# TensorE's job work behind the transposes of its step instead of ahead of its scores, in a fused top-k attention and mixture-of-experts kernel

## The chip, the cores and the metric

One core of one Trainium2 chip. The metric is device time in microseconds (us) of one execution; lower is better. TensorE is PE in the rows (PEld its weight loads), VectorE DVE, ScalarE ACT, GpSimd POOL, SyncE SP.

## What is computed

The reference is attention over 8 batches of 8 heads, 576 rows of 64, that keeps only the 32 largest scores of each row, followed by a mixture of eight experts of which each token takes one. Cut to its core:

```
scores = scale * q @ k.T
kth    = the 32nd largest score of each row
attn   = softmax(where(scores >= kth, scores, -1e9))
x      = (attn @ v), heads side by side: 4608 tokens x 512
e      = argmax(x @ w_gate)            # one expert per token
out    = gate[e] * (relu(x @ w1[e]) @ w2[e])
```

## The kernel before, in words

**Two stages.** The attention comes first, the experts' products after it, all of one program. Between them a tail finishes the last attention steps and starts the first expert.

**The attention's steps.** The score rows are cut into tiles of 128 rows; two tiles make one step, and there are 144 steps, nine (NT) for each group of four heads, eighteen for a batch. The loop at L1014 writes step t's instructions out by hand, and each engine runs its own instructions in the order in which they are written. It works on different tiles at once, as a pipeline:

- TensorE, step t: the scores of tile pair t+3 (`scores`, L367), the products with v of pair t-5 (`av`, L477 and L492), the scores' last 64 columns (`scores_left`, L380 or L386), and the transposes of the masked scores of pair t-3 (`transp`, L461).
- ScalarE, step t: the exponentials of pair t-4 out of the transposes (`exps`, L467), the sign of score minus threshold for the two tiles of pair t-2 (`softmax`, L454), between these the copy of the new scores out of PSUM (L369), then the copy of their last columns (L388).
- GpSimd, step t: the threshold of pair t-1 (`nb`, L1017) and the masking additions of pair t-2 (L455, two per step).
- VectorE, step t: the 32 largest of pair t. 21 MAX8 over pieces of the scores (L1035), then rounds of MAX8 and MATCH_REPLACE8 over the candidates (L1043).
- SyncE stores the scores and loads q, k and v.

**The jobs.** Everything else of the attention is a job, a generator that `advance` (L902) moves on at the end of a step, in the order of due times, as far as estimated costs, free PSUM banks and limits allow. The jobs are: transposing the next q and k (`j_prep`), row sums and finished rows (`j_sums`, `j_rows`), and, once per batch, finding the one row that needs a second look, doing it again and storing it (`j_find`, `j_redo`, `j_patch`), and routing the batch's tokens (`j_route`). A job does not issue its compute instructions itself; it puts them into four lists: `pq` (TensorE), `aq` (ScalarE), `dq` (VectorE), `gq` (GpSimd). `flush` (L279) empties a list into the program. The job's DMAs go out where the job stands, except those that are in a list.

So what `advance` queues at the end of step t-1 is written out as follows: `gq` at once (L1069), `pq` at L1022 of step t, between the first and the second half of `softmax` and ahead of `scores`, `aq` at L1031 behind `transp`, and `dq` between the candidate rounds of step t (L1042 to L1046, from the third instruction on, or behind them). From step 144 on L1070 to L1074 advance the jobs and empty all four lists on the spot.

**Job work that matters here.** In `j_find` VectorE makes `r_key` (from GpSimd's counts `cnt`) and `r_ok`; TensorE multiplies `r_ok` (L640); ScalarE copies the product as `stat` (L642); and, in the same step as these two, VectorE reduces `mm` (L442) for the softmax's shift. In `j_route`, for one batch before the tail, TensorE sums `hist` (L868) and VectorE makes `skip` from it in the same step (L869). In `j_rows` VectorE reads TensorE's result one step after it was queued (`xm` and `lp`, L569 and L571), and the next TensorE piece goes into the bank that this read frees. `j_redo` has VectorE make `r_wk` (L719) out of two SBUF tensors. Scores go to one of seven buffers, three steps ahead of their use.

Of the kernel before, what the change touches and what calls it, by code (L numbers as in the profile page):

```python
# [48 lines left out]
def attention_moe(ctx, tc, q, k, v, w_gate, w1, w2, out):  # L49
# [211 lines left out]
    pq, aq, dq, gq = [], [], [], []  # L261
# [9 lines left out]
    def release(pt):  # L271
        free.append(pt)
# [6 lines left out]
    def flush(queue):  # L279
        while queue:  # L280
            queue.pop(0)()
# [15 lines left out]
    def bank():  # L297
        return free.pop(0)
# [43 lines left out]
    def grp(t):  # L342
        if t < 0 or t >= steps:
            return []
        n, s = divmod(t, NT)
        p = 2 * n
        if s < MAIN:
            return [p * NT + s, p * NT + MAIN + s]
        if s == MAIN:
            return [p * NT + 2 * MAIN, (p + 1) * NT + 2 * MAIN]  # L350
        s -= MAIN + 1
        return [(p + 1) * NT + s, (p + 1) * NT + MAIN + s]

    def scores(slot):

        if not slot:
            return
        EX.append(pair())
        for n, u in enumerate(slot):
            SB[u] = EX[-1][:, n]  # L360
            p, j = divmod(u, NT)
            assert p in READY
            h, i = divmod(j, MAIN)
            w = slice(2 * LEFT + i * 128, 2 * LEFT + (i + 1) * 128) if h < 2 else slice(0, 2 * LEFT)
            r = slice(h * D, (h + 1) * D) if h < 2 else slice(0, 128)
            qk = QK[p % 3][r]
            nc.tensor.matmul(MAINS[:, n], qk[:, 0, w], qk[:, 1, 2 * LEFT:], start=True, stop=True)  # L367

        nc.scalar.activation(bass.AP(EX[-1].tensor, EX[-1].offset, [list(EX[-1].ap[0]), [S + LEFT, 2], [1, M]]), MAINS,  # L369
                             AF.Copy)  # L370
# [66 lines left out]
    def spread(pt):  # L437
        pe(nc.tensor.matmul, pt[:, 0:128], top.to_broadcast([128, 128]), ident, start=True, stop=True)

    def settle(pt, ns, done):  # L440
        mm = jobs.tile([128, 1], F32, name="mm")
        vec(nc.vector.tensor_reduce, mm, pt[:, 0:128], axis=AX.X, op=OP.max)  # L442
        vec(done)
        for n in ns:
            vec(nc.vector.scalar_tensor_tensor, shift[:, n], slope, mm, level, op0=OP.mult, op1=OP.add)
# [3 lines left out]
    def softmax(t, us, i):  # L449
        b, lt = divmod(t, 2 * NT)  # L450
        if lt == 0 and i == 0:
            CNT[b] = jobs.tile([128, NLT], F32, name="cnt")
        nb, u = NB[t], us[i]
        nc.scalar.activation(upper(SG[i]), SB[u], AF.Sign, bias=nb[:, i, 1:2], accum_out=CNT[b][:, 2 * lt + i:2 * lt + i + 1])  # L454
        nc.gpsimd.tensor_tensor(SB[u], SB[u], SG[i], op=OP.add)  # L455

    def transp(t):
        x = EX[t].rearrange("p a s -> p (a s)")
        tt = three.rearrange("p (c q) -> p c q", c=NB9)
        for c in range(NB9):  # L460
            nc.tensor.matmul(tt[:, c], x[:, c * 128:(c + 1) * 128], ident, start=True, stop=True,  # L461
                             is_transpose=True)

    def exps(t):
        ET[t] = work.tile([128, NB9, 128], F32, name="et")
        assert t // NT in SHIFTED
        nc.scalar.activation(ET[t], three.rearrange("p (c q) -> p c q", c=NB9), AF.Exp, bias=shift[:, t // NT, 0:1],  # L467
                             scale=0.125)

    def av(t, us):  # L470
        et = ET[t]

        def one(px, p, h, n, q, kbs):
            rv = VV[p // 2]
            for kb in range(kbs):
                blk = MAIN if kb == MAIN else n * (MAIN + 1) + kb
                yield lambda kb=kb, blk=blk: nc.tensor.matmul(  # L477
                    px[h * 64:(h + 1) * 64], block(rv, p % 2, kb if kb < MAIN else MAIN + n, h), et[:, blk, q],
                    start=(kb == 0), stop=(kb == KB - 1))

        def both(a, b):
            for x, y in zip(a, b):
                x()
                y()

        p, j = divmod(us[0], NT)
        if j < 2 * MAIN:
            px = PX[:, (j % 2) * 128:(j % 2 + 1) * 128]
            both(*(one(px, p, h, h, slice(0, 128), MAIN) for h in range(2)))

            o = (MAIN + 1) * D
            nc.tensor.matmul(px, VV[p // 2][:, p % 2, o:o + 2 * D], et[:, MAIN, :], start=False, stop=True)  # L492
            if p not in XT:
                XT[p] = jobs.tile([128, S], F32, name="xt", bufs=4)
            if j % 2:
                act(nc.scalar.activation, XT[p][:, (j - 1) * 128:(j + 1) * 128], PX, AF.Copy)
        else:
            XT[p + 1] = jobs.tile([128, S], F32, name="xt", bufs=4)
            for n in range(2):
                px = PX[:, n * LEFT:(n + 1) * LEFT]  # L500
                both(*(one(px, p + n, h, n, slice(h * LEFT, (h + 1) * LEFT), KB) for h in range(2)))
                act(nc.scalar.activation, XT[p + n][:, 512:S], px, AF.Copy)
# [394 lines left out]
    def start(lane, job, due=0):  # L897
        lanes[lane].append((due, job))
        if len(lanes[lane]) == 1:
            wants[lane] = next(job)  # L900
# [36 lines left out]
    def prep(p):  # L937
        if p < P:
            start(f"prep{p % 2}", j_prep(p))
# [74 lines left out]
    for t in range(steps + LAG + TD + 4):  # L1014
        n, s = divmod(t, NT)
        if delayed:
            delayed[0](*delayed[1])  # L1017
        if grp(t - LAG - TD - 1):
            exps(t - LAG - TD - 1)
        if grp(t - LAG):  # L1020
            softmax(t - LAG, grp(t - LAG), 0)
        flush(pq)  # L1022
        scores(grp(t + LA))
        if grp(t - LAG):
            softmax(t - LAG, grp(t - LAG), 1)
        if grp(t - LAG - TD - 2):
            av(t - LAG - TD - 2, grp(t - LAG - TD - 2))
        scores_left(grp(t + LA))
        if grp(t - LAG - TD):
            transp(t - LAG - TD)  # L1030
        flush(aq)  # L1031
        one, two, last = topk(t, grp(t)) if grp(t) else ([], [], None)
        for m in range(max(len(one), 1)):
            if m < len(one):
                one[m][0](*one[m][1])  # L1035
        delayed = last
        if t == 1:
            settle(first_pt, [0, 1, 2, 3], lambda: release(first_pt))
            mine_, dq[:] = dq[:], []
            flush(mine_)  # L1040
        mine, dq[:] = dq[:], []
        for m, (f, a) in enumerate(two):  # L1042
            f(*a)  # L1043
            if mine and m >= 2:
                mine.pop(0)()
        flush(mine)  # L1046
        if t == 0:
            nc.vector.tensor_reduce(top, VQ[0][:, 0:2, 0], axis=AX.X, op=OP.max)
            first_pt = bank()
            spread(first_pt)  # L1050
            pq.pop()()
        if s == NT - 1 and n in MX:
            pool(nc.gpsimd.tensor_scalar, top, MX.pop(n), top, None, op0=OP.max)
        m = t - LAG + 1
        if m > 0 and m % (2 * NT) == 0:
            start("find", j_find(m // (2 * NT) - 1), t + DUE['find'])
            start("redo", j_redo(m // (2 * NT) - 1), t + DUE['redo'])
        m = t - LAG
        if 0 <= m < steps and m % NT == NT - 1:
            start("sums", j_sums(m // NT), t + DUE['sums'])  # L1060
            if m == steps - 1 and len(lanes["sums"]) == 1:

                for _ in range(2):
                    wants["sums"] = next(lanes["sums"][0][1])
                flush(gq)
                flush(aq)
        if t < steps:
            advance(s=s)
            flush(gq)  # L1069
        else:  # L1070
            for _ in range(TAIL if t < steps + TADV else 0):
                advance(None)
                for queue in (gq, pq, aq, dq):
                    flush(queue)  # L1074
        for at, job, a in AHEAD if first else ():
            if t - steps == at:
                job(*a)
        m = t - LAG - TD - 3
        if m >= 0 and m % NT == NT - 1:
            start("rows", j_rows(m // NT), t + DUE['rows'])  # L1080
        if s == PA:
            prep(2 * n + 4)
        if s == PB:
            prep(2 * n + 3)
        if s == LQ and n + 2 < NQ:
            load_qk(n + 2)
        if s == LV and 0 < n < NQ:
            load_v(n)
# [418 lines left out]
```

## Time and profile before

| | |
|---|---|
| median of 3 runs | 1328.07 us (1327.75 to 1328.79) |
| the profiled execution | 1328.21 us, of which the profile's span is 1326.4 us |
| TensorE, VectorE busy in the span | 92%, 78% |
| GpSimd, ScalarE busy in the span | 65%, 63% |
| TensorE's mean granted clock | 0.972 of full speed |

How to read it: the span is what the profiler saw of the program; 1.8 us of the execution lie outside. Busy shares are means over the two stages, so a stage is read from its own stretch. A row of a timeline says start, length, engine, source line, operation and tiles (written <- read), how many instructions are merged, and, in brackets, how long the engine stood idle before and who released it.

### The profile page before, as it was taken

Reading aid. Unit: us, or ns where it says so; the run is one execution under the profiler, and the core shown is the slowest. Engines: PE = TensorE matmul, PEld = TensorE weight load, DVE = VectorE, ACT = ScalarE, POOL = GpSimd, SP = SyncE. Lnnn points to the kernel's source line nnn. Section 1 sums busy time; section 2 is a strip of 40 time slices with the busy share of each in tenths; the row PEclk is TensorE's granted clock in tenths of the full one; section 3 lists DMA queues with packets and bytes.
Section 4 is the critical chain, followed back from the end, with each engine's and each line's share of the span. In section 5 each row is a group of like instructions: output and inputs, shape, how many; then the busy total and the mean of one; then the engine's idle time right before and its main releaser. Section 6 shows DMA issues by size and latency. Waiting matters only on the chain.

```text
span 1326.4 us, 31779 instructions
## 1 busy us (share of the span) xinstructions
PE 1220.1 (92%) x9126; PEld 975.1 (74%) x9126; DVE 1028.7 (78%) x6889; ACT 833.8 (63%) x1691; POOL 866.6 (65%) x1317
## 2 busy tenths in 40 slices
PE   5898989989899999989988859998899999999997
PEld 2576767767667667666666657887799899988996
DVE  7998999999999999999999965644673333345665
ACT  3998888988888798888887843432233323233442
POOL 3677766877877777877877966764654334255654
PEclk8999999999999899999999978998999999999999
DMA  6655554655555556556553524635564333256774
GB/s 173 207 176 182 173 182 149 185 163 165 177 158 167 159 172 176 167 159 173 180 164 123 177 62 134 207 93 160 151 183 151 112 104 120 82 154 187 219 216 124
DMA packets 271240, 211.19 MB, mean 159 GB/s; under 512 B 136215, under 2 KB 214215, under 8 KB 271056
## 3 DMA queue, kind: packets, MB, share of 16 engines
q1 hardware_dynamic: 260320, 185.92, 47.7%
q0 software_dynamic: 9504, 22.86, 5.4%
q8 instruction: 74, 1.21, 0.4%
q14 instruction: 110, 0.90, 0.2%
q10 hardware_dynamic: 1232, 0.30, 0.1%
HBM read 102.49 MB, written 107.90 MB: 159 GB/s over the span
## 4 chain that ended last, share of the span: by engine, by line
PE 42%; DVE 33%; ACT 9%; POOL 6%; issue 5%; DMA 3%; SPq 1%; another core or an unknown queue 0%; POOLq 0%; ACTq 0%; DVEq 0%
DVE cand L1035 16%; PE ph L1169 15%; PE y L1184 14%; DVE cand L1043 6%; DVE vq L1043 5%; PE ps L367 3%; PE pt L265 3%; ACT sg L454 3%; ACT sb L369 2%; PE px L477 2%; ACT et L467 2%; POOL sb L455 2%; PE tt L461 1%; PE mt L1149 1%; POOL wl L967 1%
## 5 line engine op out<-in xcount | busy, mean ns | idle before, releaser
L455 POOL TENSOR_TENSOR sb<-sb,sg 128x576 f32<-128x576 f32 x288 | 365.5, 1282 | 87.7 <-ACT sg L454 71.8
L1035 DVE MAX8 cand<-sb 128x8 f32<-128x52 f32 (+2 forms) x3024 | 368.4, 207 | 0.9 <-ACT sb L369 0.5
L967 POOL TENSOR_TENSOR wl<-r,wh 128x512 fp32r<-128x512 f32 x110 | 142.3, 1295 | 226.1 <-DVE wh L966 221.8
L454 ACT ACTIVATE sg<-sb,nb 128x576 int8<-128x576 f32 x288 | 225.6, 783 | 5.8 <-POOL sb L455 5.2
L477 PEld LDWEIGHTS px<-et,rv 128*64 128x64 f32 x2688 | 136.7, 145 | 122.3 <-issue 59.5
L1170 ACT ACTIVATE hh<-ph 128x320 fp32r<-128x320 f32 (+3 forms) x136 | 58.3, 429 | 241.7 <-PE ph L1169 226.8
L369 ACT ACTIVATE sb<-ps 128x1024 f32<-128x1024 f32 x144 | 148.1, 1028 | 76.7 <-PE ps L367 75.7
L1043 DVE MAX8 vq<-cand 128x8 f32<-128x22 f32 (+7 forms) x1152 | 193.6, 198 | 0.3 <-DVE vq L1043 0.3
L367 PE MATMUL ps<-qk 64*128 64x512 f32 (+1 forms) x576 | 188.3, 662 | 3.0 <-ACT sb L369 2.6
L467 ACT ACTIVATE et<-tt,shift 128x1152 f32<-128x1152 f32 x144 | 177.0, 1229 | 13.9 <-PE tt L461 13.8
L1171 DVE SCALAR_TENSOR_TENSOR hl<-ph,hh 128x320 fp32r<-128x320 f32 (+3 forms) x136 | 65.1, 478 | 151.2 <-ACT hh L1170 133.3
L477 PE MATMUL px<-et,rv 128*64 128x128 f32 (+1 forms) x2688 | 170.4, 275 | 11.8 <-ACT r_et L265 7.0
L461 PE MATMUL tt<-turner,sb 128*128 128x128 f32 x1296 | 168.4, 275 | 4.3 <-POOL sb L455 3.2
L1169 PE MATMUL ph<-xh,wh 128*128 128x320 f32 (+3 forms) x536 | 168.9, 315 | 0.0
L1169 PE MATMUL ph<-xh,wl 128*128 128x320 f32 (+3 forms) x536 | 165.3, 308 | 0.0
L1169 PE MATMUL ph<-xl,wh 128*128 128x320 f32 (+3 forms) x536 | 165.3, 308 | 0.0
L461 PEld LDWEIGHTS tt<-turner,sb 128*128 128x128 f32 x1296 | 147.6, 143 | 7.1 <-POOL sb L455 4.6
L1043 DVE MATCH_REPLACE8 cand<-vq,cand 128x22 f32<-128x22 f32 (+2 forms) x864 | 148.9, 178 | 0.0
L1184 PE MATMUL y<-wh,hl 128*128 128x512 f32 x324 | 128.4, 396 | 0.0
L1184 PE MATMUL y<-wh,hh 128*128 128x512 f32 x324 | 127.7, 394 | 0.6 <-ACT yo L1188 0.6
L1184 PE MATMUL y<-wl,hh 128*128 128x512 f32 x324 | 127.9, 395 | 0.0
L1169 PEld LDWEIGHTS ph<-xh,wh 128*128 128x128 f32 x536 | 101.6, 189 | 3.8 <-issue 0.9
(266 smaller groups left out, 2235.7 us busy)
## 6 DMA issues: line engine op xcount, KB each, us to landing
r<-in_moe_w_dram SPq DMA_DIRECT2D x220, 256.0 KB
sc<-sb SPq DMA_DIRECT2D x128, 288.0 KB
sc<-sb SPq DMA_DIRECT2D x128, 256.0 KB
rv<-in_v_dram SPq DMA_DIRECT2D x32, 256.0 KB
xs<-xm SPq DMA_DIRECT2D x16, 512.0 KB
rq<-in_q_dram SPq DMA_DIRECT2D x60, 128.0 KB
rk<-in_k_dram SPq DMA_DIRECT2D x60, 128.0 KB
sc<-sb SPq DMA_DIRECT2D x32, 144.0 KB
```

Source lines behind the costliest of these rows:

```text
L367: nc.tensor.matmul(MAINS[:, n], qk[:, 0, w], qk[:, 1, 2 * LEFT:], start=True, stop=True)
L369: nc.scalar.activation(bass.AP(EX[-1].tensor, EX[-1].offset, [list(EX[-1].ap[0]), [S + LEFT, 2], [1, M]]), MAINS, AF.Copy)
L454: nc.scalar.activation(upper(SG[i]), SB[u], AF.Sign, bias=nb[:, i, 1:2], accum_out=CNT[b][:, 2 * lt + i:2 * lt + i + 1])
L455: nc.gpsimd.tensor_tensor(SB[u], SB[u], SG[i], op=OP.add)
L461: nc.tensor.matmul(tt[:, c], x[:, c * 128:(c + 1) * 128], ident, start=True, stop=True, is_transpose=True)
L467: nc.scalar.activation(ET[t], three.rearrange("p (c q) -> p c q", c=NB9), AF.Exp, bias=shift[:, t // NT, 0:1], scale=0.125)
L477: yield lambda kb=kb, blk=blk: nc.tensor.matmul(px[h * 64:(h + 1) * 64], block(rv, p % 2, kb if kb < MAIN else MAIN + n, h), et[:, blk, q] ...
L967: (nc.gpsimd if i else nc.vector).tensor_tensor(lo, r, hi, op=OP.subtract)
L1035: one[m][0](*one[m][1])
L1043: f(*a)
L1169: nc.tensor.matmul(ph, a[:, c, :], x[:, c, s], start=(m == 0), stop=(m == len(seq) - 1))
L1184: nc.tensor.matmul(PY[u, t], a[:, s], x, start=(f == 0 and m == 0), stop=(f == FC - 1 and m == 2))
```

## The change

The line that empties TensorE's list moves, within the same step, from ahead of `scores` to behind `transp`, in front of the line that empties ScalarE's. No other line changes.

```
--- before.py
+++ after.py
@@ -1019,7 +1019,6 @@
             exps(t - LAG - TD - 1)
         if grp(t - LAG):
             softmax(t - LAG, grp(t - LAG), 0)
-        flush(pq)
         scores(grp(t + LA))
         if grp(t - LAG):
             softmax(t - LAG, grp(t - LAG), 1)
@@ -1028,6 +1027,7 @@
         scores_left(grp(t + LA))
         if grp(t - LAG - TD):
             transp(t - LAG - TD)
+        flush(pq)
         flush(aq)
         one, two, last = topk(t, grp(t)) if grp(t) else ([], [], None)
         for m in range(max(len(one), 1)):
```

## Rows read from the trace of the kernel before

**Rows 1.** Busy time by stretch: us, then PE, PEld, DVE, ACT, POOL, granted clock, DMA.
```profile
450.00:500.00 50.00, 46.49 (x422) 34.68 (x420) 50.00 (x405) 45.91 (x97) 40.10 (x68) 0.97 0.59 177
...
1000.00:1326.00 326.00, 317.85 (x1875) 286.25 (x1873) 147.69 (x257) 107.48 (x217) 148.84 (x152) 0.99 0.50 147
```

**Rows 2.** Waits of VectorE, 30 to 785 us: total us, times, longest.
```profile
DVE r_key L265 <- POOL cnt L265: 6.3, 2, 5.2
DVE mm L265 <- ACT stat L265: 6.2, 6, 1.6
DVE skip L265 <- PE pt L265: 2.7, 1, 2.7
DVE cand L1035 <- ACT sb L369: 0.5, 1, 0.5
```

**Rows 3.** Timeline of the first steps, TensorE, ScalarE and VectorE.
```profile
25.26 1.07 PE L265 MATMUL pt<-turner,rq 128*128 128x128 f32 x2 [7.20 <-DMA rq<-in_q_dram]
27.30 3.62 PE L367 MATMUL ps<-qk 128*128 128x512 f32 x4
30.95 1.02 ACT L369 ACTIVATE sb<-ps 128x1024 f32<-128x1024 f32 x1 [12.30 <-PE ps L367]
33.17 0.78 ACT L454 ACTIVATE sg<-sb,nb 128x576 int8<-128x576 f32 x1
```

**Rows 4.** Timeline around the two waits of r_key.
```profile
108.83 1.28 POOL L455 TENSOR_TENSOR sb<-sb,sg 128x576 f32<-128x576 f32 x1 [0.68 <-ACT sg L454]
113.86 0.20 DVE L265 SCALAR_TENSOR_TENSOR r_key<-cnt,idx 128x36 f32<-128x36 f32 x1 [5.18 <-POOL cnt L265]
...
199.62 1.28 POOL L455 TENSOR_TENSOR sb<-sb,sg 128x576 f32<-128x576 f32 x1 [1.95 <-ACT sg L454]
206.62 0.20 DVE L265 SCALAR_TENSOR_TENSOR r_key<-cnt,idx 128x36 f32<-128x36 f32 x1 [1.11 <-POOL cnt L265]
```

**Rows 5.** Waits of ScalarE, 32 to 109 us and then 109 to 781 us.
```profile
ACT sb L369 <- PE ps L367: 1.4, 2, 1.2
...
ACT sb L369 <- PE ps L367: 58.0, 40, 4.0
```

**Rows 6.** Timeline of one job step in which TensorE waits for VectorE.
```profile
382.89 1.18 PE L265 MATMUL pt<-turner,xt 128*128 128x144 f32 x8 [2.45 <-DVE lp L265]
386.45 1.02 ACT L369 ACTIVATE sb<-ps 128x1024 f32<-128x1024 f32 x1 [3.02 <-PE ps L367]
```

**Rows 7.** Timeline, one of the six mm chains: product, stat, mm.
```profile
400.56 0.18 PE L265 MATMUL pt<-r_ok,before 128*128 128x1 bf16 x1 [0.72 <-DVE r_ok L265]
405.25 0.17 ACT L265 ACTIVATE stat<-pt 128x3 f32<-128x3 f32 x1
405.45 0.29 DVE L265 TENSOR_REDUCE mm<-pt 128x1 f32<-128x128 f32 x1 [0.81 <-ACT stat L265]
```

**Rows 8.** Timeline of TensorE, scores of two steps with no job between.
```profile
115.03 1.13 PE L367 MATMUL ps<-qk 64*128 64x512 f32 x4
118.73 1.13 PE L367 MATMUL ps<-qk 64*128 64x512 f32 x4
```

**Rows 9.** Timeline around the wait of skip.
```profile
721.11 0.18 PE L265 MATMUL pt<-hist,ones 128*128 128x8 bf16 x1
721.35 0.16 DVE L265 TENSOR_SCALAR skip<-pt 128x1 f32<-128x1 f32 x1 [2.74 <-PE pt L265]
```

**Rows 10.** Instructions on tile r_wk: ns min/median/max; then the longest, in the timeline.
```profile
L265 DVE TENSOR_TENSOR r_wk<-sg,r_sb x8: 748/1022/5418, 182.4 to 836.6; 128x576 f32<-128x576 bf16 x8
...
763.22 2.52 POOL L455 TENSOR_TENSOR sb<-sb,sg 128x576 f32<-128x576 f32 x2
763.56 5.42 DVE L265 TENSOR_TENSOR r_wk<-sg,r_sb 128x576 f32<-128x576 bf16 x1
765.84 2.52 POOL L455 TENSOR_TENSOR sb<-sb,sg 128x576 f32<-128x576 f32 x2
```

**Rows 11.** Timeline of TensorE, the first instructions of the experts' stage.
```profile
806.63 0.63 PE L1149 MATMUL mt<-turner,kt 128*128 128x128 f32 x4
```

More of the change, by code (lines that the diff above doesn't have):

```diff
@@ L1021, in attention_moe @@
             softmax(t - LAG, grp(t - LAG), 0)
-        flush(pq)
         scores(grp(t + LA))
@@ L1030, in attention_moe @@
             transp(t - LAG - TD)
+        flush(pq)
         flush(aq)
```

## The prediction

> **What bounds the kernel now.** I read the busy time by stretch first. In the attention VectorE is busy 50.00 of 50 us, TensorE 46.5, ScalarE 45.9, GpSimd 40.1; in the experts' stage TensorE is, with 318 of 326 us [rows 1]. So the attention's length is VectorE's work and VectorE's waits, whatever TensorE gains by itself. The change touches TensorE's list alone, and that list is used this way only in the attention; the experts' stage, which begins at 806.6 us [rows 11], can only be shifted. Next I read VectorE's own waits. Between 30 and 785 us they are 6.3 us in two waits for GpSimd's counts, 6.2 us in six waits of `mm`, 2.7 us in one wait of `skip`, and 0.5 us, once, for scores [rows 2]. These 15.7 us are what a better order can win on VectorE directly. That scores were late only once also tells that bringing scores earlier, which is what the change does in each step, is worth nothing by that way: they stand ready in their buffers. Last I read what sets each of these waits, in the timelines.
>
> **The change part by part.** Nothing is added or removed: the same TensorE instructions, the same on every other engine, no DMA moved. TensorE has, in turn, a step's own work S and job work P, before and after. What shifts is which P stands between two S: it is now one S later. A step without jobs lasts 118.73 - 115.03 = 3.7 us [rows 8], so each P comes some 3.7 us later beside its S, and each S earlier by the P and the waits that stood ahead of it. What P waits for (VectorE's and ScalarE's job work of the step before) gets 3.7 us of slack; what waits for P in its own step loses 3.7.
>
> 1. The start, 0.5 us won. In step 1 the job's transposes wait 7.2 us for a load, and the scores stand behind them: they start at 27.30, ScalarE stands 12.3 us for them, and its first sign, at 33.17, comes only behind that [rows 3]. Now the scores go ahead of the wait. The transposes still end at 27.3, ScalarE's job copy of them follows (half as wide as the 1.02 us copy in these rows, so some 0.6 us), and the first sign starts near 28, some 5.2 us earlier. VectorE's 0.5 us wait for scores [rows 2] falls here and goes. Bounds: 0 and 0.5.
>
> 2. The waits of `r_key`, 5.5 us won. The first is 5.18 us at 113.86 and ends when GpSimd has made the counts; GpSimd's addition ahead of them, at 108.83, waited for ScalarE's sign [rows 4]. Between 32 and 109 us ScalarE waits only 1.4 us for scores [rows 5]: it is full and never makes up for its late start. So its 5.2 us of step 1 arrive whole, and nearly all of the 5.18 goes. The second, 1.11 us, hangs on an addition that waited 1.95 us for ScalarE [rows 4], and ScalarE waits 58 us for scores in the rest of the attention [rows 5]. I take 0.4 of it. Bounds: 0 (GpSimd late on its own account) and 6.3.
>
> 3. TensorE's waits in P, nothing won by themselves. In the job step shown TensorE waits 2.45 us for VectorE's reading of the bank, and ScalarE 3.02 us for the scores behind it [rows 6]. This goes; what hides it is VectorE, which is full. It matters through items 2 and 4 alone: ScalarE and GpSimd come earlier. Next late, in ScalarE's steps, are then its own copies of P, which now wait for P. The exponentials behind them must wait for the transposes ahead of P anyway, so the copies cost P and themselves on ScalarE; VectorE's lead in scores [rows 2] covers that. If the cover were gone, it would be up to the 3.0 us that ScalarE loses in [rows 6], in each such step.
>
> 4. `mm`, 3 us won. The product of `r_ok` stands in P, `stat` in ScalarE's list, `mm` behind it, all in one step. Here 4.7 us lie between the product and `stat` (405.25 - 400.56, the shortest of the six) [rows 7], because ScalarE's turn comes late, so 3.7 us more for P are covered with 1.0 to spare: no loss. How much earlier ScalarE's turn comes the trace does not show. Bounds: all 6.2 us won, or 3 us lost, if TensorE's step ends half a microsecond behind ScalarE's turn at each of the six. I take half the 6.2, since the lead of item 3 is as large as the single waits but is not had at each of the six.
>
> 5. `skip`, 1 us lost. Here nothing covers: TensorE's product is at 721.11, `skip` at 721.35, after 2.74 us of waiting [rows 9]. P one S later would make it 3.7 us longer; as TensorE has lost its waits by then, up to the whole 2.74 could go instead. I take 1 us of loss, nearer to the uncovered end. Behind the waiting instruction stand the rest of VectorE's selection and all its later steps, so it counts in full.
>
> 6. VectorE's stretched instructions, 1 us won. `r_wk` takes 748 ns at best, 1022 at the median and 5418 once, at 763.56, where GpSimd's four additions run without a gap from 763.22 to 768.36 [rows 10]. GpSimd comes earlier, so the same block should lie partly ahead of `r_wk`. Bounds for this one: 4.7 us won, nothing. The other stretched ones get a new phase each, of either sign; I take zero.
>
> The sum: -0.5 - 5.5 - 3 + 1 - 1 = -9.0 us on VectorE. The tail hangs on VectorE's end and the experts on the tail, so it goes through. Against the profiled execution of 1328.2 us (span 1326.4 and 1.8 outside), which is 0.1 above the median, this gives **1319.2 us**.
>
> **The rivals.** *A, nothing to measure, about 1327.6.* GpSimd's late counts come from its own work, `mm` from ScalarE's turn, and the gains stay on engines that do not bound: only the 0.5 us of item 1 is left. For it: VectorE is full [rows 1], TensorE is not. Against it: the late start of ScalarE [rows 3] is as large as the first wait of `r_key` [rows 4], and ScalarE has no gap in which the lag could come from elsewhere [rows 5].
>
> *B, slower, about 1337.* When ScalarE no longer waits between its two signs, GpSimd's two additions of a step follow each other without a gap, 2.5 us instead of twice 1.25 [rows 10], and VectorE's job instructions on two SBUF tensors stand still for the whole of it, as `r_wk` did for 5.42 us. The place is the redo, find and route work of VectorE, some four such instructions in each of seven batches. If half of them are stopped for one more addition of 1.25 us, that is 7 x 2 x 1.25 = 17.5 us, less the 9.0 above: +8.5. It comes out as slower from (9.0 + 2.7) / 7 = 1.7 us per batch. Against it: with GpSimd nearer to VectorE's pace its additions fall on the MAX8 of the next step, where the trace shows no stretch. The Trainium skill (SBUF — State Buffer, "SBUF: two separate sides") says that VectorE and GpSimd share one pair of SBUF ports under an exclusive lock, held for a whole instruction, so that the loser blocks fully. The trace agrees in the 5.42 us; by that rule B's 17.5 us come or stay away with the alignment of the two engines.
>
> *C, larger, about 1310.* All of the 15.7 us of waits but the 2.7 of `skip`, and the 4.7 of `r_wk`, go: 13.0 + 4.7 = 17.7. It needs ScalarE ahead at all six `mm`.
>
> **How the numbers follow.** A measurement of this kernel tells about 0.2%, 2.7 us, from no change: faster is below 1325.4, slower above 1330.7. My forecast with C has 0.68 (C 0.10 of it), A 0.18, B 0.14. The range goes from C, 1309, to 1331: A lies in it, and of B the part in which the stalls just outweigh the gain; what is left out is most of B and the gains beyond C.
>
> **What would show it.** Step 1: scores near 18 and the first sign near 28 us. `r_key` without its 5.18 us; waits of VectorE for GpSimd under 1 us. The waits of TensorE for `lp` gone, and ScalarE's 58 us for scores down to a fraction. `mm` at or below 0.8 us each, `skip` near 3.7. `r_wk` at 763 (now some 8 us earlier) below 5 us. The experts' stage begins near 798 and lasts as long as before. I am wrong if `r_key` still waits with the first sign at 28 (then GpSimd bounds it), if `mm` waits for TensorE rather than for ScalarE, if VectorE's job instructions get longer in sum by more than 9 us (B), or if the tail between VectorE's last selection and the experts grows by what the attention won.

## The result and the profile after

The changed kernel takes 1312.16 us (median of 4 runs, 1308.99 to 1314.04) against 1328.43 (4 runs, 1327.75 to 1330.23) beside it: a ratio of 0.9873, interval 0.985 to 0.9897, or 16.3 us. The prediction was 1319.2, 9.0 us less than before. The profiled execution of the changed kernel took 1314.04 us with a span of 1312.2, that is 14.2 less than the span before.

The attention is where it went. VectorE's last selection starts, with its 21 MAX8 over the scores (L1035), at 771.79 us before (first line) and at 756.39 after (second line), 15.4 us earlier:
```profile
771.79 2.56 DVE L1035 MAX8 cand<-sb 128x8 f32<-128x52 f32 x21
756.39 2.56 DVE L1035 MAX8 cand<-sb 128x8 f32<-128x52 f32 x21
```
The tail and the experts only follow: TensorE's first instruction of the experts' stage comes 15.9 us earlier [rows 11], and the time between those two points is nearly the same in both (34.8 us and 34.3). The experts' stage itself lasts 521.5 us, 1.7 more than before, so that 14.2 of the 15.9 us are left in the span.

The start, TensorE and ScalarE, in the timeline of the changed kernel:
```profile
18.45 1.98 PE L367 MATMUL ps<-qk 128*128 128x512 f32 x4 [0.48 <-ACT sb L369]
25.14 0.96 PE L265 MATMUL pt<-turner,rq 128*128 128x128 f32 x2 [3.87 <-DMA rq<-in_q_dram]
28.15 0.77 ACT L454 ACTIVATE sg<-sb,nb 128x576 int8<-128x576 f32 x1
...
790.70 1.09 PE L1149 MATMUL mt<-turner,kt 128*128 128x128 f32 x4
```
The scores now go ahead of the wait for `rq`, and the first sign stands at 28.15 instead of 33.17 [rows 3]. They also take 1.98 us instead of 3.62: before, they came behind TensorE's wait of 7.2 us, and the granted clock was 0.5 there, that is 1.2 GHz instead of 2.4.

VectorE's waits, 30 to 785 us, and the row of the longest one (columns as in [rows 2]):
```profile
DVE r_key L265 <- POOL cnt L265: 8.6, 2, 7.2
DVE skip L265 <- PE pt L265: 5.3, 1, 5.3
...
DVE mm L265 <- ACT stat L265: 2.2, 1, 2.2
...
773.49 0.20 DVE L265 SCALAR_TENSOR_TENSOR r_key<-cnt,idx 128x36 f32<-128x36 f32 x1 [7.21 <-POOL cnt L265]
```
The 7.21 us lie at 773, behind the last selection: that is the tail, which the earlier end only drew into the window. In the attention itself 1.36 (`r_key`) + 5.34 (`skip`) + 2.15 (`mm`) = 8.9 us of waiting are left of 15.7 [rows 2].

What the other two engines wait for, from the waits of ScalarE (109 to 770 us) and of TensorE (30 to 770 us):
```profile
ACT sg L454 <- POOL sb L455: 53.2, 42, 5.0
...
PE tt L461 <- POOL sb L455: 24.0, 36, 4.3
```
The waits have mostly changed their name. ScalarE's 58 us for scores [rows 5] have become 53 us for GpSimd's additions, and TensorE's 24 us for `lp` (one of these waits in [rows 6]) have become 24 us for the same additions. The two engines are little less idle than before: from 30 us to VectorE's last selection ScalarE stands 92 us instead of 102, TensorE 53 instead of 62. They are *earlier* against VectorE, and now stand in front of GpSimd.

TensorE's waits had a second price, its clock. Between the start and VectorE's last selection the granted clock of the kernel before falls to 0.5 (1.2 GHz) eight times; seven of these times begin within 2 us behind a wait of TensorE of 2.2 to 2.7 us, five of the waits being for `lp` (four more such waits were followed by no fall). In the changed kernel it falls once. No run separates the clock's share in the gain; a high clock alone is not enough for it: the run with a longer TensorE (below) has a mean granted clock of 0.984, above the 0.981 of the changed kernel, and is 13 us slower than that.

Out of one batch's chain from `r_key` to `mm`, in the timeline of the changed kernel:
```profile
294.23 2.53 POOL L455 TENSOR_TENSOR sb<-sb,sg 128x576 f32<-128x576 f32 x2
295.67 1.13 DVE L265 SCALAR_TENSOR_TENSOR r_key<-cnt,idx 128x36 f32<-128x36 f32 x1
298.81 0.17 ACT L265 ACTIVATE stat<-pt 128x3 f32<-128x3 f32 x1
301.32 0.28 DVE L265 TENSOR_REDUCE mm<-pt 128x1 f32<-128x128 f32 x1
301.77 0.36 DVE L265 SCALAR_TENSOR_TENSOR shift<-slope,mm,level 128x3 f32<-128x3 f32 x1
```
`stat` is 2.5 us ahead of `mm`, where before `mm` stood waiting for it [rows 7]. But `r_key`, which needs 0.20 us [rows 4], takes 1.13 here. It ends at 296.80; GpSimd's two additions, which follow each other without a gap, end at 296.76. Before, the same thing happened to other instructions, as in the timeline of the kernel before behind the `mm` of [rows 7]:
```profile
405.84 0.80 POOL L265 TENSOR_TENSOR vq<-vq 128x288 f32<-128x288 f32 x1
...
405.91 0.75 DVE L265 SCALAR_TENSOR_TENSOR shift<-slope,mm,level 128x3 f32<-128x3 f32 x1
```
`shift` ends at 406.66, the GpSimd operation at 406.64. So there are two accounts on VectorE, waits and lengthened instructions. I added up the 389 job instructions of VectorE (L265) between 30 us and its last selection in each timeline: 136.5 us before, 129.1 after. Those that are more than 0.08 us longer than the shortest of their kind, 42 before and 37 after, all end at one short distance behind the end of a GpSimd operation: 0.06 us or less, `hist` 0.2, `r_wk` 0.6.

| VectorE, us (negative is a gain) | forecast | measured |
|---|---|---|
| start (wait for scores) | -0.5 | -0.5 |
| waits of `r_key` | -5.5 | -4.9 (5.18 to 1.36, 1.11 to none) |
| waits of `mm` | -3 | -4.0 (6.2 to 2.2) |
| wait of `skip` | +1 | +2.6 (2.74 to 5.34) |
| length of the job instructions | -1 | -7.4 |
| the rest of the 15.4 | | -1.2 |

The measured figures are of one execution of each kernel. The first wait of `r_key`, 1.36 us here, is 2.53 us in the run with `skip` covered (below), whose program is the same up to there.

The last measured line but one is made of +4.9 for `r_key` (six batches at 1.1 us), -3.2 for `r_wk`, -3.2 for `pos`, -2.0 for `r_v`'s first, -1.9 for `shift`, -1.0 for `r_fl`, -0.9 for `sh`, and smaller ones.

`skip` and the `r_wk` of the last batch, in the timeline of the changed kernel:
```profile
700.96 2.57 PE L461 MATMUL tt<-turner,sb 128*128 128x128 f32 x9 [4.28 <-POOL sb L455]
704.72 2.08 PE L367 MATMUL ps<-qk 64*128 64x512 f32 x4
710.02 0.18 PE L265 MATMUL pt<-hist,ones 128*128 128x8 bf16 x1
710.30 0.16 DVE L265 TENSOR_SCALAR skip<-pt 128x1 f32<-128x1 f32 x1 [5.34 <-PE pt L265]
...
750.44 2.52 POOL L455 TENSOR_TENSOR sb<-sb,sg 128x576 f32<-128x576 f32 x2
752.34 1.23 DVE L265 TENSOR_TENSOR r_wk<-sg,r_sb 128x576 f32<-128x576 bf16 x1
```
The product for `skip` stands behind a whole step of TensorE's own work, 5.3 us from 704.72 to 710.02, and VectorE waits for all of it. About 1 us of this step is the clock: behind TensorE's wait of 4.28 us for GpSimd's additions the granted clock is 0.5 from 700 to 706 us, and the scores take 2.08 us where they take 1.13 at 2.4 GHz [rows 8]. `r_wk` now comes 0.6 us before the end of GpSimd's additions instead of at their beginning [rows 10], so it loses 0.5 us where it lost 4.7.

### The profile page after: what moved, and what is told of

It reads as the page before. It is cut to its first block, busy times and chain, and to the rows that moved or that the text cites. A ratio compares the mean times of both kernels' runs of the same rounds, so it can differ in the third digit from the quotient of the medians.

```text
span 1312.2 us, 31782 instructions
## 1 busy us (share of the span) xinstructions
PE 1218.0 (93%) x9126; PEld 969.5 (74%) x9126; DVE 1021.8 (78%) x6889; ACT 831.2 (63%) x1691; POOL 865.1 (66%) x1317
## 4 chain that ended last, share of the span: by engine, by line
DVE 40%; PE 37%; POOL 7%; issue 6%; ACT 6%; DMA 2%; SPq 1%; POOLq 0%; ACTq 0%; DVEq 0%
DVE cand L1035 19%; PE ph L1169 15%; PE y L1184 15%; DVE cand L1043 8%; DVE vq L1043 7%; POOL sb L455 2%; ACT sg L454 2%; PE pt L265 2%; PE mt L1149 1%; PE ps L367 1%; POOL wl L967 1%; ACT sb L369 1%; POOL table L857 1%; PE tt L461 1%; PE px L477 1%
## 5 line engine op out<-in xcount | busy, mean ns | idle before, releaser
L1035 DVE MAX8 cand<-sb 128x8 f32<-128x52 f32 (+2 forms) x3024 | 368.6, 208 | 0.3 <-issue 0.2
L477 PEld LDWEIGHTS px<-et,rv 128*64 128x64 f32 x2688 | 130.6, 138 | 124.3 <-ACT xt L265 47.8
L461 PE MATMUL tt<-turner,sb 128*128 128x128 f32 x1296 | 176.5, 277 | 27.4 <-POOL sb L455 24.0
L367 PE MATMUL ps<-qk 64*128 64x512 f32 (+1 forms) x576 | 184.0, 647 | 4.8 <-ACT sb L369 3.5
L1171 DVE SCALAR_TENSOR_TENSOR hl<-ph,hh 128x320 fp32r<-128x320 f32 (+3 forms) x136 | 65.1, 479 | 152.5 <-ACT hh L1170 129.1
L477 PE MATMUL px<-et,rv 128*64 128x128 f32 (+1 forms) x2688 | 164.0, 268 | 15.7 <-ACT xt L265 7.8
```

The lines of the kernel that those rows point to most:

```text
L477: yield lambda kb=kb, blk=blk: nc.tensor.matmul(px[h * 64:(h + 1) * 64], block(rv, p % 2, kb if kb < MAIN else MAIN + n, h), et[:, blk, q] ...
```

## The experiments

Theory: TensorE's own time in the attention is worth nothing; the change moves the instants at which ScalarE and GpSimd come, and thereby VectorE's waits and the GpSimd operations that VectorE's instructions meet. The rival, in several forms: TensorE's steps got shorter (by its clock too), or one part (the start, one kind of job) carries everything. The kernel before ran beside each group of runs; its medians were 1329.14 (the first four), 1328.23 (the next four), 1328.85 (three) and 1327.71 (the last).

### What the start is worth

The late place in step 1 alone:
```
-        flush(pq)
+        if t != 1:
+            flush(pq)
         scores(grp(t + LA))
...
             transp(t - LAG - TD)
+        flush(pq)
```


> The list is emptied late in step 1 alone, early in all others. Theory 1 (the start's lead is one part, the other steps the larger part): the first sign near 28 us, the first wait of r_key down from 5.2 to about 1.4 us, VectorE's 0.5 us wait for scores gone, but the six mm waits (6.2 us), the 2.7 us of skip and the 5.4 us r_wk as before: 1323 to 1325 us. Theory 2 (the start's lead carries on through the whole attention and is nearly all of the gain): mm waits and the long r_wk go too, 1312 to 1317 us.

Measured: 1326.81 us, ratio 0.9974 (0.9959 to 0.999). Below the expected gain: `r_key` still waited 4.89 us. Timeline of this run, TensorE, ScalarE and VectorE:
```profile
28.75 0.77 ACT L454 ACTIVATE sg<-sb,nb 128x576 int8<-128x576 f32 x1
...
31.17 0.48 PE L265 MATMUL pt<-turner,rk 128*128 128x128 f32 x1 [0.70 <-DMA rk<-in_k_dram]
31.95 2.08 PE L367 MATMUL ps<-qk 64*128 64x512 f32 x4
...
34.08 1.02 ACT L369 ACTIVATE sb<-ps 128x1024 f32<-128x1024 f32 x1 [4.48 <-PE ps L367]
```
The first sign did come early. But in step 2 the old order held again, and so two portions of job work, step 1's transposes of `rq` and step 2's of `rk` with their loads, stand one behind the other ahead of step 2's scores; these come at 31.95 instead of 27.55 in the changed kernel, ScalarE stands 4.48 us, and what was won is given back one step later. The edit had not separated what it was meant to separate.

The complement, early in step 1 alone and late everywhere else (`if t == 1:` in the same place):

> The list is emptied early in step 1 alone, late in all others. Theory 1: the first sign stays near 33 us and r_key's first wait at 4 to 5 us, but from the second batch on no mm wait, and r_wk no longer 5.4 us: 1315 to 1318 us. Theory 2: little is won, 1324 us or more.

Measured: 1315.57 us, ratio 0.9887 (0.9865 to 0.9909): the first theory's number. The waits of VectorE show where the missing start is paid:
```profile
DVE r_key L265 <- POOL cnt L265: 9.7, 2, 7.2
DVE skip L265 <- PE pt L265: 5.5, 1, 5.5
DVE xm L265 <- ACT sg L454: 3.1, 1, 3.1
DVE mm L265 <- ACT stat L265: 2.2, 1, 2.2
```
`xm` waits 3.1 us for ScalarE's sign, and `r_key` 2.5 (9.7 less the 7.2 of the tail). All five later waits of `mm` are gone without the early start: they come from the later steps.

So the start was tried once more, late in steps 0 to 3; step 3 has no job work, so the two orders meet without harm:
```
+        if t >= 4:
+            flush(pq)
         scores(grp(t + LA))
```


> The kernel before, with the job work behind the masked scores' transposes in steps 0 to 3 alone; step 3 has no job work, so that the two orders meet where no two portions of job work stand in front of one step's scores. Theory (the late start of ScalarE is carried whole to the first counts): first sign near 28 us, first wait of r_key near 1.4 us instead of 5.2, the first mm some 1 us later, everything behind as before: 3.3 us less on VectorE, 1324 to 1327 us. Rival one (ScalarE's lag at 109 us is made by the steps between, not by the start): r_key still waits 4 us or more, 1327.5 us or more. Rival two (an early start is worth more than that, as ScalarE then leads in all later batches too): under 1321 us, and the later mm do not wait.

Measured: 1321.43 us, ratio 0.9943 (0.9921 to 0.9965), 6.8 less than the 1328.23 beside it: twice the expected 3.3, and only 0.4 us above the band of rival two. Timeline of ScalarE and VectorE, then a row of VectorE's waits (30 to 785 us):
```profile
28.64 0.77 ACT L454 ACTIVATE sg<-sb,nb 128x576 int8<-128x576 f32 x1
...
100.91 0.77 ACT L454 ACTIVATE sg<-sb,nb 128x576 int8<-128x576 f32 x1
...
108.81 0.20 DVE L265 SCALAR_TENSOR_TENSOR r_key<-cnt,idx 128x36 f32<-128x36 f32 x1 [0.61 <-POOL cnt L265]
...
DVE mm L265 <- ACT stat L265: 5.4, 6, 1.2
```
The lead of 4.5 us at the first sign is 5.0 at 100.91 (before, that sign stands at 105.94): ScalarE does carry its start whole to the first counts, and 4.6 of the 5.18 us go. The six `mm` still wait 5.4 us, so rival two falls by its second sign: the early start does nothing for the `mm` of the later batches. The attention's VectorE is 7.2 us earlier in this profile; 5.1 of it are the two steps with the start and the first `r_key`, the rest small differences of several steps.

### Which job work, and how late

The rows job's TensorE work alone late, all other jobs' in the old place (a second list for the lane "rows"):
```
+    rowsq, running = [], [None]
+    def pe(f, *a, **k):
+        (rowsq if running[0] == "rows" else pq).append(lambda: f(*a, **k))
...
             transp(t - LAG - TD)
+        flush(rowsq)
```


> Only the TensorE work of the finished rows (the job that waits for VectorE's reading of lp) comes late, that of all other jobs early as before the change. Theory (what counts from the second batch on is that TensorE no longer waits for VectorE in front of the scores, 24 us in 12 waits before): these waits go, ScalarE and GpSimd run ahead, five of the six mm waits fall under 0.3 us each, skip stays near 2.7 us or falls, the start stays as before: 1316 to 1321 us. Rival (it is the place of find's and redo's TensorE work that counts): mm waits stay at 0.8 us or more, 1325 us or more.

Measured: 1335.64 us, ratio 1.0051 (1.0032 to 1.0069): slower than before. The expectation fell, and both signs of the rival came (`mm` at 0.8 us or more, over 1325 us). Waits of TensorE (with one of them in the timeline), of ScalarE (both 109 to 770 us) and of VectorE (30 to 785) in this run:
```profile
PE pt L271 <- DVE lp L265: 28.3, 10, 3.3
...
293.49 1.11 PE L271 MATMUL pt<-turner,rq 128*128 128x128 f32 x4 [3.28 <-DVE lp L265]
...
ACT sb L373 <- PE ps L371: 59.0, 34, 5.3
...
DVE mm L265 <- ACT stat L265: 10.4, 6, 2.6
```
TensorE's waits for `lp` are as long as before, but other work has them. VectorE's making of `lp` frees a PSUM bank. Before, nine of the twelve waits were of the rows' own products (the one in [rows 6] among them); here all ten are of the next q's transposes, another job's, which still stand ahead of the scores and go into that bank. So TensorE still waits ahead of the scores as long as the waiting piece stands there, whichever piece that is. ScalarE waits 59 us for scores, as before, and `mm` 10.4 instead of 6.2. The rival, that the place of the find and redo work counts, is not excluded by this: no run moved that work alone. Against it stands that before the change find's product was ready 4.7 us and more ahead of `stat` [rows 7]: it was ScalarE's turn that came late, not that product.

All job work behind the scores, but ahead of the transposes (with `skip` covered, as in the next section):
```
+        flush(pq)
         if grp(t - LAG - TD):
             transp(t - LAG - TD)
-        flush(pq)
```


> The changed kernel with the wait of skip covered by a step, and the job work ahead of the masked scores' transposes instead of behind them, still behind the scores. TensorE waits 24 us in all for GpSimd's additions in front of those transposes; the job work now fills that. Theory (TensorE's own waits are worth nothing, VectorE is the bound, and what helped was the scores ahead of the job work): 1307 to 1312 us, the same as with skip covered alone. Rival (TensorE's shorter step is what brings ScalarE and GpSimd forward): 1305 us or less.

Measured: 1313.8 us, ratio 0.9889 (0.9872 to 0.9906), against 0.9848 with `skip` covered alone: 5 us worse than that, and 2 us above the expected band. The rival's way is excluded. What the theory missed are ScalarE's exponentials, which now wait for the transposes. Waits of ScalarE, 109 to 770 us:
```profile
ACT et L467 <- PE tt L461: 45.4, 56, 2.1
```
With `skip` covered alone these are 3.0 us. That the 5 us come from there is not shown: ScalarE is no more idle in sum, VectorE's last selection comes 2.3 us later (1.1 of them in the first `r_key`), and 1.3 us more fall in the experts' stage, which the edit does not touch. Behind the transposes is the better of the two late places by the medians; the intervals just overlap.

### What skip costs

The changed kernel, with the product of `hist` and `skip` a step apart:
```
             pe(nc.tensor.matmul, pt[:, 0:E], ones, hist[:, :, KB], start=True, stop=True)
+            yield need(slack=1)
             vec(nc.vector.tensor_scalar, skip[:, w], pt[:, w], -1.0, float(T * 128), op0=OP.mult, op1=OP.add)
```


> The changed kernel, with VectorE's skip put one step behind the TensorE product that it reads, not in the same step. Theory (skip is the one consumer in the same step that nothing covers): its 5.3 us wait goes whole and VectorE is bound there: 5 us less than the changed kernel measured beside it, 1306 to 1308 us at a median of 1312. Rival (the wait only takes the place of another one that GpSimd's late work would cause anyway): less than 2 us won.

Measured: 1309.53 us, ratio 0.9848 (0.982 to 0.9877), some 3 us below the changed kernel's ratio, between the theory's 1306 to 1308 and the rival's "less than 2 us"; the intervals overlap. In the profile the effect is plain: the 5.34 us are now
```profile
DVE skip L265 <- PE pt L265: 0.2, 1, 0.2
```
and VectorE's last selection starts at 754.31, 2.1 us earlier than in the changed kernel. The gain is less than 5.1 us because `r_v` (2.0) and `ebase` (0.7) in the last batches met GpSimd at another point, and because the first `r_key` waited 1.2 us longer, in a stretch that the edit does not touch.

### Who sets the pace

TensorE lengthened: four of the nine transposes of `transp` made twice, with the same values.
```
-        for c in range(NB9):
+        for c in (0, 1, 2, 3) + tuple(range(NB9)):
```


> The changed kernel, with four of the nine transposes of the masked scores made twice in each of the 144 steps (the same values written again). Nine take 1.15 us, so this adds some 0.4 us a step, about 60 us of TensorE's time in the attention. Theory (VectorE is the bound, TensorE's time in the attention is worth nothing by itself): 1312 to 1318 us, VectorE's waits for TensorE or ScalarE up by less than 4 us. Rival (the change won because TensorE's steps got shorter, so TensorE's length counts): 1340 us or more.

Measured: 1325.25 us, ratio 0.9974 (0.9953 to 0.9995): 13 us more than the changed kernel's ratio gives, twice the upper end that I expected, and far from the rival's 1340. Waits of VectorE, 30 to 785 us:
```profile
DVE mm L265 <- ACT stat L265: 6.5, 3, 3.0
DVE xm L265 <- PE pt L265: 3.8, 1, 3.8
DVE skip L265 <- PE pt L265: 3.6, 1, 3.6
DVE r_key L265 <- POOL cnt L265: 3.4, 1, 3.4
```
The transposes take 56 us more on TensorE (232.4 us of busy time instead of 176.5), and three quarters of that are hidden. The rest comes out on VectorE's two accounts: about 9 us as waits, mostly the old ones, and 5.3 us as longer job instructions. So TensorE does not set the pace alone, but its time is not worth nothing either: its cover is thin (46.49 of 50 us busy before [rows 1]).

VectorE lengthened by one MAX8 on constants per step, and, in a second kernel, by one scalar_tensor_tensor on constants at the same place:
```
+        if one:
+            nc.vector.max(filler[:, 0], filler[:, 1])
```
```
+        if one:
+            nc.vector.scalar_tensor_tensor(filler[:, 0], filler[:, 1], 1.0, filler[:, 2],
+                                           op0=OP.mult, op1=OP.add)
```


> The changed kernel, with one MAX8 of 128x8 on a constant tile more on VectorE in each step, behind the 21 MAX8 over the scores. Two such instructions of the selection take 0.31 us, overlapped, so one is about 0.1 us: 144 x 0.1 = 14 us. Theory (VectorE's time is the attention's time): 1322 to 1329 us. Rival (VectorE has slack that its busy share hides): under 1317 us. No MAX8 is longer in the trace when GpSimd works, so none of the 144 is expected over 0.2 us.

> As the run with one MAX8 more, at the same place, but the added instruction is a scalar_tensor_tensor of 128x8 on two constant tiles. Theory (such an instruction stands still until the GpSimd operation under way ends): in the trace of the changed kernel a GpSimd operation covers that place in 118 of 144 steps, and what is left of it there sums to 53 us; as the engines shift against each other when VectorE gets slower, 25 to 55 us over the run with the MAX8, so 1345 to 1385 us, and each long one ends within 0.1 us of the end of a GpSimd operation. Rival (the long job instructions have another reason, their own operands or the queue): the same time as the run with the MAX8 within 10 us.

Measured: 1315.18 us, ratio 0.9895 (0.9865 to 0.9925), for the MAX8, and 1348.93 us, ratio 1.0144 (1.0112 to 1.0176), for the other. The groups of these instructions by form, from 20 us on, where 142 of the 144 lie (columns: busy us, mean ns of one, idle before them), the first of the MAX8's run, the rest of the other's:
```profile
L1040 DVE MAX8 filler<-filler 128x8 f32<-128x8 f32 x142 | 21.5, 151 | 0.0
```
```profile
L1040 DVE SCALAR_TENSOR_TENSOR filler<-filler 128x8 f32<-128x8 f32 x142 | 72.1, 507 | 0.0
...
330.58 1.05 POOL L267 TENSOR_TENSOR r_xa<-r_xa,r_hm 128x512 f32<-128x512 f32 x1
331.58 0.20 POOL L1019 TENSOR_TENSOR nb<-vq,factors 128x4 f32<-128x4 f32 x1
331.74 2.50 POOL L457 TENSOR_TENSOR sb<-sb,sg 128x576 f32<-128x576 f32 x2
330.82 3.44 DVE L1040 SCALAR_TENSOR_TENSOR filler<-filler 128x8 f32<-128x8 f32 x1
...
764.28 2.52 POOL L457 TENSOR_TENSOR sb<-sb,sg 128x576 f32<-128x576 f32 x2
764.83 0.76 DVE L1040 SCALAR_TENSOR_TENSOR filler<-filler 128x8 f32<-128x8 f32 x1
```
The same place, the same size: 0.15 us against 0.51 on average. In the timeline 100 of the 144 are longer than 0.25 us, and each of the 100 ends within 0.1 us of the end of a GpSimd operation; no MAX8 is longer than 0.16. How many operations they stand through differs: four of them stand through four (the 3.44 us), but a third get their turn after the first although the next follows without a gap, as at 764.83, where the instruction ends at 765.59, between the two additions. What decides this no run here shows. The sums differ by 72.1 - 21.5 = 50.6 us (expected 53), the times by 33.75 us: the rest came back, since `r_key`, `mm` and `r_fl` were no longer held or waiting (`r_fl` 1.9 to 0.15 in four batches, `r_key` 1.1 to 0.18 in six). This is the theory's case, and the rival's 10 us are excluded. What is not as I expected is the MAX8's price: with 1315.18 us the run lies in the band of its rival ("VectorE has slack", under 1317), and its interval overlaps that of the changed kernel. The profile tells the two apart: the instructions overlap, a plain step grows from 4.48 to 4.54 us, 144 x 0.06 = 8.6 us, and shorter job instructions gave back 5.1 of these (`r_wk` alone 3.0) and the waits some more, to leave 3.2 us at VectorE's last selection. So the price is in VectorE's steps, and was given back by the second account; the time alone does not show it.

The Trainium skill (SBUF — State Buffer, "SBUF: two separate sides") has the shared port pair go to whichever starts first, a GpSimd operation that reads SBUF or a VectorE instruction with two SBUF inputs, for that whole instruction. The blocking agrees with these rows; "whichever starts first" does not cover the 3.44 us, in which GpSimd ran four operations one after another before VectorE got its turn, while the 0.76 us are as it says.

### Another place for VectorE's job instructions

If the lengths are a matter of meeting GpSimd, the place of the job instructions in VectorE's step should matter. In the changed kernel with `skip` covered, from the seventh instruction of the later selection on, instead of the third:
```
-            if mine and m >= 2:
+            if mine and m >= 6:
```


> The changed kernel with the wait of skip covered by a step, and VectorE's job instructions placed between the later instructions of the selection, from the seventh on instead of the third. In the trace of the changed kernel r_key starts at 295.67, behind the third, and stands until 296.80, when GpSimd's two additions end at 296.76; the seventh is some 0.5 us later. Theory (what is long there is waiting for GpSimd's operation, so a later place is cheaper): r_key 0.5 us shorter in six batches, shift and the find stage's first ones too, 2 to 5 us less than with skip covered alone, that is 1304.5 to 1307.5 us. Rival (what VectorE does not wait for there it waits for later, or the later results delay the next step): 1309 us or more.

Measured: 1297.87 us, ratio 0.9778 (0.9758 to 0.9797): 9 us less than the ratio with `skip` covered alone, better than expected, and the fastest kernel of the study, 31 us below the kernel before. In the profiles 8.2 us of the difference lie at VectorE's last selection; the experts' stage, which the edit does not touch, is 3.8 us shorter besides. Timeline of GpSimd and VectorE:
```profile
292.82 2.52 POOL L455 TENSOR_TENSOR sb<-sb,sg 128x576 f32<-128x576 f32 x2
...
294.81 0.58 DVE L265 SCALAR_TENSOR_TENSOR r_key<-cnt,idx 128x36 f32<-128x36 f32 x1
```
`r_key` now starts 0.5 us before the end of the additions and takes 0.58 instead of 1.1, as expected. `hist` (0.82 to 0.33 in four batches) and `r_wk` (0.2 to 0.6 us less in five batches, 1.1 more in the last) change by the same way; the 389 job instructions take 122.0 us instead of 130.9.

As late as they fit (`if mine and m >= 2 and len(two) - m <= len(mine):`):

> As the run before it, but the job instructions of a step are placed as late as they fit: with k of them, between the last k of the selection's 14 instructions, none behind them. r_key would start at about 296.8, when the additions are over. Theory: the six r_key without their 0.9 us, shift at 0.2, some of r_fl's 1.9 us gone, 4 to 10 us less than with skip covered alone, 1299.5 to 1305.5 us. Rival (GpSimd's next thresholds and additions, which start as soon as the selection ends, catch them instead): 1309 us or more, with instructions held by two additions, 2.5 us.

Measured: 1302.85 us, ratio 0.9808 (0.9788 to 0.9828): in the expected band, and worse than the run before it. `r_key` is at its 0.2 us, and `r_fl` lost its 1.9, but now the step's last ones meet the next additions, as the rival had it. Timeline of VectorE and GpSimd:
```profile
311.35 2.51 POOL L455 TENSOR_TENSOR sb<-sb,sg 128x576 f32<-128x576 f32 x2
...
311.63 1.02 DVE L265 SCALAR_TENSOR_TENSOR r_sl<-slots,stat,r_ok 128x8 bf16<-128x8 bf16 x1
...
312.73 2.22 DVE L265 TENSOR_TENSOR r_qx<-slots,r_sl 128x1024 bf16<-128x1024 bf16 x1
```
`r_qx` needs 1.22 us and starts when 1.1 us of the additions are left.

The same place (`m >= 6`) in the kernel before, with TensorE's old order:

> The kernel before, its order of TensorE's work kept, with VectorE's job instructions placed from the seventh instruction of the later selection on instead of the third. Theory (the place is worth what GpSimd's two additions, which follow each other without a gap once ScalarE is early, cover of it): with the order kept, GpSimd's additions come apart and later, r_key is not long to begin with (0.2 us in four of seven batches), and the additions that make shift (0.75) and pos (0.95) long come about 3 us later in the step; a place 0.5 us later meets them at another point, with either sign: 1322 to 1331 us, a gain of less than half the 11.7 us that it brought behind the moved work. Rival (the later place is worth the same whatever the order, as the early part of the selection always lies under the additions): 1314 to 1320 us.

Measured: 1326.73 us against 1327.71, ratio 1.0004 (0.9986 to 1.0022): no difference. The later place pays only behind the moved work. A reason that fits, not shown by a run of its own: there the two additions of a step follow each other without a gap in 114 of the 144 steps, in the kernel before in 85, and `r_key` is long in six batches instead of two.

## Why the prediction was right, and what it mis-sized

The direction and the mechanism of the waits held: forecast at -8.0 in sum, they came to -6.8. The mis-sized term is the sixth, the length of VectorE's job instructions: -1 forecast, -7.4 measured. Of the 7 us by which the gain exceeds the forecast this term is nearly all. Of its 7.4 us `r_wk` has 3.2, which was forecast in kind; for the other 4.2 nothing in the forecast gave the sign, so that they came out as a gain was luck.

1. The start: right (first sign 28.15, "near 28"). What the forecast did not see is the clock: the scores of step 1 were slow as well as late (3.62 us, now 1.98).
2. `r_key`: the mechanism is shown. Late until step 4 alone takes the first wait from 5.18 to 0.61 with a lead that is whole at 100.9 us. In the changed kernel 1.36 is left. Late job work in the later steps may cost ScalarE some time there: with the sign at 100.83 nearly the same, the second one behind it comes at 108.00, against 106.34 in the run with late work in the first steps only. That would be the cost that step 3 set at nothing; as another execution had 2.53 us in this place, it is not more than likely. The second wait went whole, where I took 0.4 of 1.11.
3. TensorE's waits for `lp` are gone, and 24 us of others stand in their place: right that they are worth nothing as such. The run with the rows job alone shows that moving that job's work is not enough.
4. `mm`: -4.0 for -3. Five of six waits are gone, since `stat` comes 2.5 us ahead; the sixth, 2.15 us, stands in the step behind the first `r_key`.
5. `skip`: the sign was right, the size was not: +2.6 for +1. I had let TensorE's lost waits pay for part of the step that now stands ahead; the trace shows that step whole, and longer than the 3.7 us of [rows 8], in part because TensorE's clock had fallen.
6. `r_wk`: I took 1 of the 4.7 us at stake, and 4.2 came (5.42 to 1.23). For all the others I had "a new phase each, of either sign; I take zero". The new phase is not drawn anew each time: it is much the same in most batches (`r_key` long in six of seven, `shift` shorter in five of six, `pos` in four of five), so that a change of half a microsecond in one place comes four to six times. `pos`, `shift`, `r_v`, `r_fl` and `sh` became 9 us shorter together, `r_key` 4.9 longer.

Of the rivals, A fell with the first wait. B's mechanism is real, and the scalar_tensor_tensor in every step shows it to be dear: 34 us more than a MAX8 in its place. Here it costs 4.9 us, in `r_key`, which belongs to the find work that B named. It did not decide, since the other instructions became shorter by more. The argument against it, that the additions move back under the 21 MAX8, which do not stand still, held in small part only: of the additions' 369 us 207 lie under these MAX8, 178 before, and what is left of the GpSimd operation under way at the end of the MAX8 is 52 us in 144 steps in the changed kernel and 53 before. C's size, 17.7, was the nearest to the measured 16.3, but not its way: of C's 13.0 us of waits 9.4 came, of its 4.7 in `r_wk` 4.2, and `skip` took 2.6 of these back.

The span falls by 14.2 us and the median by 16.3 because the profiled execution is the longest of its four, 1.9 us above their median. What goes with the range of 5 us is TensorE's mean granted clock: 0.981 and 0.980 in the two longer executions, 0.983 in the two shorter; and among 18 executions of the kernel before, from 0.976 at 1322.16 us to 0.965 at 1333.81. What stays open is which of the two makes the other, and how much of each account on VectorE is due to the clock.

## What to carry to other kernels

When one engine is full, add up two accounts on it, its waits and the lengths of its equal instructions against their shortest; a reordering elsewhere moves both, and here the two were about equal. A piece of work that waits belongs behind the work that others wait for, and all such pieces must move: moving the work of one job only handed the wait to another. Once the order has settled, ask which short instructions of VectorE on SBUF operands start while GpSimd works: half a microsecond of delay in their place was worth 8 to 9 us, and nothing in the order before.

## What the runs showed of the hardware

- A scalar_tensor_tensor, tensor_tensor or tensor_scalar of VectorE on SBUF operands that meets a GpSimd arithmetic operation stands at least until that operation's end: 100 of 144 instructions of 0.15 us, all within 0.1 us of such an end. It can stand through several that follow without a gap, 3.44 us over four operations (four times, each over the same four), but need not: in a third of the 100 it got its turn between two.
- MAX8 is not held: 144 of 144 at the same place took 0.14 to 0.16 us. Neither is `mm`, which reads PSUM: 0.27 to 0.29 us in every batch of both kernels.
- An added instruction cost less than its length: a MAX8 of 0.15 us adds 0.06 us to VectorE's plain step.
- TensorE's granted clock fell to 0.5 behind its waits: in the attention of the kernel before, seven of the eight falls begin within 2 us behind a wait of 2.2 to 2.7 us; other such waits were followed by none.
